# The last 128 columns of the final token block as a piece of their own, accumulated at the very end

## The chip, the cores and the metric

The kernel runs on one core of one Trainium2 chip. The time is the device time of one execution in microseconds (us), as the median of several executions. The profile's span is about 1.8 us shorter than the device time of the same execution, because it counts from the first to the last recorded instruction.

Ratios are the mean time of one kernel's runs over the mean time of the other's runs of the same rounds, so they are not quite the ratios of the medians that stand beside them.

## The reference

A linear attention (8 batches, 8 heads, 576 tokens, head size 64) feeds an MLP with a swish activation. The change touches only the last product of the MLP.

```python
kv  = einsum('bhsd,bhse->bhde', softmax_over_s(k), v)
x   = einsum('bhsd,bhde->bhse', softmax_over_d(q), kv)   # -> 4608 tokens x 512
h   = x @ w_in                                           # 512 -> 2048
g   = h * sigmoid(beta * h)
out = g @ w_out                                          # 2048 -> 512, float32
```

## The kernel before

Tokens are handled in blocks of 512 (R = 4 groups of 128 rows). For each block, 16 units of 128 hidden features (NJ = 16) each go through four matmuls into an h bank (a bank is one piece of PSUM, the memory into which matmuls write), a tanh on ScalarE, a product on VectorE that gives `g`, and then the second product: each unit adds `g` times `w_out` into accumulators of 512 columns. In the last block (LASTC), units 0 to 7 (HOLD = 8) are added inside the loop, and units 8 to 15 at the end, one accumulator after the other, so that the copies and stores of the first accumulators lie beside the matmuls of the later ones. The fourth group of rows is split into two accumulators of 256 columns, so that the last copy and the last store are half as large:

```python
def mm_b(c, j, sts=None):
    acc = acc_tiles(c)            # last block: 5 accumulators, acc[3] and acc[4] for the 4th row group
    ...
        if c == LASTC and st >= R - 1:
            hw = DM // 2          # 256 columns
            nc.tensor.matmul(acc[st][:, 0:hw], g[:, ds((R - 1) * P, P)],
                             w_out_b[:, j, ds((st - R + 1) * hw, hw)],
                             start=(j == 0), stop=(j == NJ - 1))
    ...
def store(c, st):                 # last block, st >= R - 1
    k_ = st - R + 1
    cols = ds(k_ * hw, hw)
    evac((nc.vector, nc.scalar)[k_], o[:, R - 1, cols], acc[st][:, 0:hw])
    (nc.sync, nc.scalar)[k_].dma_start(ov[:, R - 1, cols], o[:, R - 1, cols])
...
# after the loop: units 8 to 15 of each accumulator of the last block
for st in range(1, R + 1):
    for j in range(HOLD + (st == 1), NJ):
        mm_b(LASTC, j, [st])
    store(LASTC, st)
```

The softmax here doesn't subtract the row's maximum and nothing guards it: scores larger than these inputs give would overflow.

## Time and profile before

| | before |
|---|---|
| device time, median (first three runs) | 282.67 us (281.89 to 282.89) |
| span of the profiled run | 280.6 us |
| TensorE busy | 275.9 us, 98% |
| last matmul's end | 277.45 us |
| last matmul's end to the end of the span ("the tail") | 3.13 us |

The first rows say that TensorE sets the time. In the profile lines of this document, L and a number is a line of the kernel that was run, an arrow points from what is read to what is written, "x16" counts instructions, and PEld is the weight load that goes ahead of each matmul. The view lines for this kernel stand in the prediction below.

### The profile page before, as it was taken

The numbers are of one execution on the slowest core, as the hardware profiler recorded it, in microseconds if no ns is written. First come the engines' busy times: TensorE is split into PE (matmuls) and PEld (weight loads), VectorE is DVE, ScalarE is ACT, GpSimd is POOL, SyncE is SP. The second block draws the span as 40 slices with busy tenths as digits, with TensorE's granted clock in tenths as the row PEclk, the third lists the DMA queues.
The fourth block names the chain that finished last, engine by engine and source line by source line (L and its number), as shares of the span: only waits on it lengthen the run. The fifth ranks groups of instructions, "written<-read, shape, count | busy, mean of one in ns | idle before, by whom it ended". The sixth has DMA issues, their size and how long they took to land.

```text
span 280.6 us, 4450 instructions
## 1 busy us (share of the span) xinstructions
PE 275.9 (98%) x1728; PEld 128.6 (46%) x1728; DVE 175.1 (62%) x284; ACT 162.8 (58%) x248; POOL 38.7 (14%) x58
## 2 busy tenths in 40 slices
PE   8999999999999999999999999999999999999995
PEld 2544454444444444444444444444444544445543
DVE  3864796994478446945595549553864596354361
ACT  4667985958486447744684559444733574454451
POOL 1554236133030003000300030000000000000000
PEclk9999999999999999999999999999999999999999
DMA  7999999999981993199418951641154034005003
GB/s 249 390 394 391 387 388 311 321 292 213 269 240 46 238 287 90 75 233 265 141 78 191 280 167 75 132 94 79 71 89 139 1 151 75 0 0 152 0 0 150
DMA packets 55172, 50.09 MB, mean 179 GB/s; under 512 B 26600, under 2 KB 47344, under 8 KB 55152
## 3 DMA queue, kind: packets, MB, share of 16 engines
q1 hardware_dynamic: 54224, 48.91, 59.8%
q10 hardware_dynamic: 928, 0.92, 0.9%
q8 instruction: 13, 0.21, 0.3%
q14 instruction: 7, 0.06, 0.1%
HBM read 36.71 MB, written 9.44 MB: 164 GB/s over the span
## 4 chain that ended last, share of the span: by engine, by line
PE 98%; DVE 1%; ACT 0%; issue 0%
PE h L403 44%; PE acc L452 43%; PE warm L531 3%; PE kv L341 2%; PE x L372 1%; PE acc L444 1%; PE kv L316 1%; PE x L388 1%; PE tp L297 1%; DVE eq L267 0%; DVE qsT L173 0%; ACT o L171 0%; DVE xT L612 0%; PE x L363 0%; PE tb L564 0%
## 5 line engine op out<-in xcount | busy, mean ns | idle before, releaser
L417 DVE SCALAR_TENSOR_TENSOR g<-th,h 128x512 bf16<-128x512 bf16 x144 | 96.2, 681 | 80.1 <-ACT th L413 79.8
L413 ACT ACTIVATE th<-h,beta_t 128x512 bf16<-128x512 f32 x144 | 97.9, 687 | 81.9 <-PE h L403 81.0
L403 PE MATMUL h<-xT,w_in_b 128*128 128x512 bf16 x576 | 143.2, 379 | 0.0
L452 PE MATMUL acc<-w_out_b,g 128*128 128x512 bf16 x560 | 141.0, 379 | 0.0
L403 PEld LDWEIGHTS <-w_in_b 128*128 128x128 bf16 x576 | 56.3, 98 | 66.4 <-ACT w_in_b L171 0.6
L452 PEld LDWEIGHTS <-g 128*128 128x128 bf16 x560 | 53.8, 98 | 66.0 <-issue 2.5
L173 POOL CAST va<-v_st 128x2048 bf16<-128x2048 f32 (+2 forms) x14 | 17.4, 1257 | 115.2 <-DMA v_st<-in_v_dram 115.2
L261 DVE TENSOR_REDUCE rq<-eq 128x16 f32<-128x1024 bf16 (+1 forms) x20 | 22.1, 1104 | 5.6 <-ACT eq L250 5.1
L267 DVE TENSOR_TENSOR eq<-eq,rq 128x1024 bf16<-128x1024 bf16 (+1 forms) x20 | 23.1, 1157 | 0.1
L171 ACT CAST xT<-x 128x512 bf16<-128x512 f32 x18 | 9.9, 588 | 17.8 <-PE x L372 14.9
L250 ACT ACTIVATE eq<-q_st 128x1024 bf16<-128x1024 f32 (+1 forms) x18 | 16.9, 955 | 2.9 <-DMA q_st<-in_q_dram 2.9
L173 DVE COPY o<-acc 128x512 f32<-128x512 f32 (+1 forms) x19 | 12.3, 660 | 3.6 <-PE acc L452 3.4
L171 ACT COPY o<-acc 128x512 f32<-128x512 f32 (+1 forms) x18 | 9.6, 577 | 8.4 <-PE acc L452 5.0
L173 DVE CAST xT<-x 128x512 bf16<-128x512 f32 x18 | 11.5, 684 | 2.5 <-PE x L372 1.8
L192 ACT ACTIVATE ek<-k_st 128x1024 bf16<-128x1024 f32 x12 | 12.6, 1051 | 0.0
L531 PE MATMUL warm<-xT 128*128 128x512 bf16 x30 | 10.0, 493 | 1.2 <-DVE xT L612 1.2
L173 POOL CAST w_in_b<-w_in 128x512 bf16<-128x512 f32 (+1 forms) x9 | 5.9, 663 | 4.9 <-DMA w_in<-in_moe_w_in_dram 4.7
L531 PEld LDWEIGHTS <-xT 128*128 128x128 bf16 x30 | 3.5, 122 | 6.1 <-issue 3.8
L173 POOL CAST w_out_b<-w_out 128x1024 bf16<-128x1024 f32 x5 | 5.2, 1041 | 7.4 <-DMA w_out<-in_moe_w_out_dram 7.4
L262 DVE RECIPROCAL rq<-rq 128x16 f32<-128x16 f32 (+1 forms) x20 | 4.9, 243 | 0.7
L341 PEld LDWEIGHTS <-ek 128*64 128x64 bf16 x192 | 4.1, 111 | 2.5 <-issue 2.5
L185 ACT ACTIVATE ek<-k_st 128x576 bf16<-128x576 f32 x8 | 5.1, 677 | 0.2 <-DMA k_st<-in_k_dram 0.2
(48 smaller groups left out, 83.1 us busy)
## 6 DMA issues: line engine op xcount, KB each, us to landing
out_dram<-o SPq DMA_DIRECT2D x14, 512.0 KB, 3.4
q_st<-in_q_dram SPq DMA_DIRECT2D x25, 256.0 KB, 4.2
k_st<-in_k_dram SPq DMA_DIRECT2D x6, 1024.0 KB, 9.2
v_st<-in_v_dram SPq DMA_DIRECT2D x6, 1024.0 KB, 11.3
w_in<-in_moe_w_in_dram SPq DMA_DIRECT2D x6, 512.0 KB, 9.6
v_st<-in_v_dram SPq DMA_DIRECT2D x8, 288.0 KB, 8.3
w_out<-in_moe_w_out_dram SPq DMA_DIRECT2D x4, 512.0 KB, 9.0
w_out<-in_moe_w_out_dram SPq DMA_DIRECT2D x2, 1024.0 KB, 9.3
```

The source lines that it names most:

```text
L171: eng.copy(dst, src)
L173: eng.tensor_copy(dst, src)
L192: nc.scalar.activation(ek[b][:, :, h, :].rearrange("p i h d -> p h i d"), k_st[b][:, h, 0 : R * D].rearrange("p h (i d) -> p h i d", i=R), ...
L250: nc.scalar.activation(eq[b][:, :, s * m : (s + 1) * m, :].rearrange("p i h d -> p h i d"), q_st[b][:, s * m : (s + 1) * m, :].rearrange(" ...
L261: nc.vector.tensor_reduce(rq[b][:, 0, :, h], eq[b][:, :, h, :], axis=AX.X, op=ALU.add)
L267: eng.tensor_tensor(eq[b][:, :, h, :], eq[b][:, :, h, :], rq[b][:, 1, :, h].unsqueeze(3).to_broadcast((P, R, m, D)), ALU.mult,)
L341: nc.tensor.matmul(t[r * D : (r + 1) * D, j, :], ek[b][:, i, hd, :] if i < R else ekt[(b // 2) % 2][:, ds(hd * D, D)], va[b][:, i, hd, :] ...
L403: nc.tensor.matmul(h[:], w_unit(j, kt), x_of(c)[:, kt, :], start=(kt == 0), stop=(kt == KT - 1),)
L413: nc.scalar.activation(th[:], h_of[c, j][:], ACTF.Tanh, scale=beta_t[:, j : j + 1])
L417: nc.vector.scalar_tensor_tensor(out=g[:], in0=th_of.pop((c, j))[:], scalar=1.0, in1=h_of[c, j][:], op0=ALU.add, op1=ALU.mult)
L452: nc.tensor.matmul(acc[st][:], g[:, ds(st * P, P)], w_out_b[:, j, :], start=(j == 0), stop=(j == NJ - 1),)
L531: nc.tensor.matmul(t[:], xT[2][:, 0, 0:P], xT[2][:, 0, :])
```

## The change

The intent is to make the work after the last matmul smaller. The fourth row group is divided into 256, 128 and 128 columns. The last 128 are not accumulated in the loop at all: when everything else is done, all 16 units are added at once in a bank that held h tiles and is free by then, and the result is copied by ScalarE and stored from ScalarE's queue. While those matmuls run, the store ahead can leave.

```diff
+    ENDS = ((0, DM // 2), (DM // 2, DM // 4), (3 * DM // 4, DM // 4))
@@ mm_b
-                hw = DM // 2
+                lo, hw = ENDS[st - R + 1]
...
-                    w_out_b[:, j, ds((st - R + 1) * hw, hw)],
+                    w_out_b[:, j, ds(lo, hw)],
@@ store
-                hw = DM // 2
-                k_ = st - R + 1
-                cols = ds(k_ * hw, hw)
-                evac((nc.vector, nc.scalar)[k_], o[:, R - 1, cols], acc[st][:, 0:hw])
-                (nc.sync, nc.scalar)[k_].dma_start(ov[:, R - 1, cols], o[:, R - 1, cols])
+                lo, hw = ENDS[st - R + 1]
+                cols = ds(lo, hw)
+                last = st == R - 2 + len(ENDS)
+                evac(nc.scalar if last else nc.vector, o[:, R - 1, cols], acc[st][:, 0:hw])
+                (nc.scalar if last else nc.sync).dma_start(ov[:, R - 1, cols], o[:, R - 1, cols])
@@ the end
-    for st in range(1, R + 1):
-        for j in range(HOLD + (st == 1), NJ):
+    for st in range(1, R + 2):
+        if st > R:
+            acc_of[LASTC].append(ps.tile([P, DM], F32, tag=bank("h"), bufs=1, name=f"acc{LASTC}_{st}"))
+        for j in range(HOLD + (st == 1) if st <= R else 0, NJ):
             mm_b(LASTC, j, [st])
```

## The prediction

> **What bounds the kernel now.** I read the page's busy table first, then the chain that ended last, then the groups by form, then the timeline of the last 5 us, and last the stretches of the final store. The page and the chain, in order of time, say that one engine sets the time from start to end:
>
> ```profile
> PE 275.9 (98%) x1728; PEld 128.6 (46%) x1728; DVE 175.1 (62%) x284; ACT 162.8 (58%) x248; POOL 38.7 (14%) x58
> ...
> PE 98%; DVE 1%; ACT 0%; issue 0%
> ...
> 265.34 5.18 PE h L403 x24
> 270.52 5.18 PE acc L452 x24
> 275.70 1.76 PE acc L444 x16
> ```
>
> The first line is busy time, the second the chain by engine, the rest the end of the chain (start, length, count). TensorE is busy for 98% of a span of 280.6 us, and it is also what the chain runs through. So a change is worth what it takes off the matmul stream, plus what it takes off the stretch after the last matmul. That stretch is the target of the change, and the timeline has it:
>
> ```profile
> 275.54 1.91 PE L444 MATMUL acc<-w_out_b,g 128*128 128x256 bf16 x16
> 275.74 0.69 DVE L173 COPY o<-acc 128x512 f32<-128x512 f32 x1 [2.55 <-PE acc L452]
> 276.46 0.33 SPq L515 DMA_DIRECT2D out_dram<-o  x1
> 276.62 0.42 DVE L173 COPY o<-acc 128x256 f32<-128x256 f32 x1 [0.18 <-PE acc L444]
> 277.07 0.33 SPq L512 DMA_DIRECT2D out_dram<-o  x1
> 277.49 0.37 ACT L171 COPY o<-acc 128x256 f32<-128x256 f32 x1 [2.89 <-PE acc L444]
> ...
> 277.89 0.36 ACTq L512 DMA_DIRECT2D out_dram<-o  x1
> ```
>
> The last matmul ends at 275.54 + 1.91 = 277.45. ScalarE copies its 128x256 half from 277.49 to 277.86, its queue issues the store at 277.89, and the DMA list gives 1.8 us from that issue to landing, which is 279.7. The last 0.9 us to 280.6 is the ending of the program. So the tail after the last matmul is 280.6 - 277.45 = 3.15 us. This is 1.1% of the span: even its whole removal wouldn't reach the 2% line, 5.65 us.
>
> **What the Trainium skill says.** "TensorE: Matmul & The Clock Gate", section "Back-to-back issue gap", has N/2.4 + 2.5 ns for a warm matmul of N columns, but also says that a real stream of weight load and matmul pairs sustains about 81 ns at N=128. The two differ for the new matmuls: 55.8 against 81. This trace agrees with the formula at N=256: the 16 matmuls above span 1.91 us with a last one of 273 ns, so (1.91 - 0.273)/15 = 109 ns each, and the formula has 109.2. At N=128 with a fresh 128x128 weight load each, the trace has the transposes of L297, and at N=64 the L363 group:
>
> ```profile
> 40.45 0.45 PEld L297 LDWEIGHTS <-eq 128*128 128x128 bf16 x8
> 40.45 0.62 PE L297 MATMUL tp<-identity,eq 128*128 128x128 bf16 x8
> ...
> 217.90 0.40 PE L363 MATMUL x<-qsT,kvp 128*128 128x64 bf16 x8
> ```
>
> (0.62 - 0.219)/7 = 57 ns, and (0.40 - 0.193)/7 = 30 ns, where 219 and 193 ns are one instruction of each from the groups by form. So the trace agrees with the formula, not with 81; and full weight loads that alternate with 64-column matmuls keep up with 30 ns although one is recorded as 98 ns long. I take 56 ns. "DMA: Bandwidth & Descriptors", section "Anatomy of one DMA", puts a fixed ~2.0 us on a DMA, most of it the write receipt, independent of size (for the GpSimd path); the trace has 1.8 us for the final 128 KB store on ScalarE's queue, of the same order. The same page, section "Why small descriptors are slow", gives about 3 cycles of overhead on top of one per 32 bytes, for the packet cost used below.
>
> **The change part by part.** The last token block's fourth quarter of rows used to be two accumulators of 256 columns, each accumulated for units 0 to 7 inside the main loop and for 8 to 15 at the end. Now it is 256, 128 and 128 columns; the last 128 are taken out of the loop and done for all 16 units at the very end, in an h bank. The built instruction order shows 32 more TensorE rows (16 weight loads, 16 matmuls) and the new group last.
>
> Removed on TensorE: the second accumulator's 16 matmuls narrow from 256 to 128 columns, 8 in the loop and 8 at the end: 16 x (109 - 56) = 0.85 us. The loop part, 8 x 53 = 0.42 us, counts in full only if TensorE doesn't wait there; the stretches 250 to 260 and 260 to 270 us show it busy 10.00 of 10.00 us each.
> Added on TensorE: 16 matmuls of 128 columns, 16 x 56 = 0.90 us.
> Sum: +0.05 us by these rounded figures. The total number of columns is the same; what is added is 16 times the fixed 2.5 ns, 0.04 us. The last matmul itself records 219 instead of 273 ns, but that is already in the pace. So TensorE ends at about 277.5, against 277.45.
>
> Last copy: 128x128 instead of 128x256 on ScalarE. The groups by form have both sizes on each engine:
>
> ```profile
> L171 ACT COPY o<-acc 128x512 f32<-128x512 f32 x17 | 9.3, 589 | 5.5 <-PE acc L452 5.0
> ...
> L171 ACT COPY o<-acc 128x256 f32<-128x256 f32 x1 | 0.4, 372 | 2.9 <-PE acc L444 2.9
> ...
> L173 DVE COPY o<-acc 128x512 f32<-128x512 f32 x18 | 11.9, 673 | 3.4 <-PE acc L452 3.4
> ...
> L173 DVE COPY o<-acc 128x256 f32<-128x256 f32 x1 | 0.4, 425 | 0.2 <-PE acc L444 0.2
> ```
>
> ScalarE: 256 columns cost 589 - 372 = 217 ns, so 128 more or fewer cost 108, and the new copy is 372 - 108 = 264 ns, estimated. On the path: -0.11 us. VectorE's new 128-column copy is about 425 - 124 = 301 ns; it lies beside the 0.9 us of new matmuls and is off the path.
>
> Last store: 64 KB in 512-byte rows instead of 128 KB in 1024-byte rows. In stretches of 0.1 us the old one shows as
>
> ```profile
> 278.70:278.80 0.10, 0.00 (x0) 1.00 0.22 82
> 278.80:278.90 0.10, 0.00 (x0) 1.00 0.90 328
> 278.90:279.00 0.10, 0.00 (x0) 1.00 0.98 358
> 279.00:279.10 0.10, 0.00 (x0) 1.00 0.98 358
> 279.10:279.20 0.10, 0.00 (x0) 1.00 0.50 164
> 279.20:279.30 0.10, 0.00 (x0) 1.00 0.08 21
> ```
>
> where the last two columns are the share of the 16 DMA engines and GB/s. The shares sum to 3.66 tenths, 0.37 us of each engine. By the skill's packet rule 1024 bytes are 32 + 3 = 35 cycles and 512 bytes 16 + 3 = 19, so the new store needs 0.37 x 19/35 = 0.20 us, an estimate: -0.17 us. The issue before it (0.8 us) and the receipt behind it (about 0.4 us) stay.
>
> The earlier stores don't collide. The 128 columns taken out of the loop move the ends of the other accumulators 0.42 us forward. The third one's copy then ends near 276.6 and the fourth's (128 columns on VectorE) near 276.95, so the sync queue issues at about 276.65 and 277.0, and the last issue, on ScalarE's queue, comes at about 277.8. Before, the last two issues were 277.07 and 277.89.
>
> Sum on the path: +0.05 (matmuls) - 0.11 (copy) - 0.17 (store) = -0.23 us. One more store has its completion waited for at the end, perhaps +0.03. So about -0.2 us: 282.67 - 0.2 = 282.45.
>
> **The rivals.** *First, weight loads become the pace.* If 32 matmuls of 128 columns run at the skill's sustained 81 ns, they cost 32 x 25 = 0.8 us more, and the time is about 283.25; at the recorded 98 ns of a load it is 32 x 42 = 1.3 us, 283.8. For it: the weight load's record, and the skill's figure for such streams. Against it: the transposes' 57 ns and the 30 ns at 64 columns. One chance in ten.
> *Second, a wait for the new bank.* The new accumulator takes a bank that held an h tile, and its first matmul must wait until ScalarE and VectorE have read that tile. The last such read ends at 271.97 in the timeline (the last g), and the new group begins near 276.6: 4.6 us of slack, so this wait should be nothing. Nor should the operands bind: the last group needs the 16 g tiles of the block, and the last of these is the same one. If the bank did bind for a reason that the profile doesn't show, it would cost a few tenths. One in twenty.
> *Third, the gain is wholly hidden.* If the end is set by fixed store latency, halving the last store returns nothing beyond the copy, and an extra completion at the end costs a little: 282.6. The stretches speak for part of this: 0.2 us of about 1.8 us from issue to landing is all that depends on size. One in four. All these differ by less than the three runs of before do among themselves (281.89 to 282.89), so the total alone will hardly tell them apart; the profile should.
>
> **Range and chances.** The centre is 282.45. The mechanisms span -0.25 to +1.1 us, mostly below zero; the spread of runs adds half a microsecond either way to a median. I take 281.8 to 283.1. For 2% the time would have to leave 277.0 to 288.3, and no mechanism here comes near: faster 0.005, same 0.99, slower 0.005.
>
> **What would show it.** Right: in the profile of after, the 128x128 matmuls of the second line of accumulators number 32 and their last 24 span 23 x 56 + 219 = 1.5 us; no idle time of TensorE before them; TensorE's end within 0.1 us of 277.5; the last ScalarE copy about 264 ns; the last store landing about 1.6 us after its issue; and a span of about 280.4. Wrong: a 24-group of 2.1 us or more (weight loads bind), a wait ahead of the new accumulator's first weight load (the bank), a last landing of 1.8 us or more (fixed latency), or a loop that doesn't get its 0.42 us shorter. A total outside the range with these lines all as foretold would mean that the end of the program, after the last landing, has changed.

## The result and the profile after

The changed kernel took 281.98 us (median of four, 281.92 to 282.13) against 282.50 us of the kernel before in the same rounds (281.89 to 282.89). The ratio is 0.9984, with a 95% interval of 0.9965 to 1.0004. That is within 2% by far, and the interval still holds 1. The predicted 282.45 us is 0.47 us above the median, and inside the range.

Busy times and the chain by engine, from the page of the changed kernel:

```profile
PE 275.6 (98%) x1744; PEld 128.7 (46%) x1744; DVE 175.3 (63%) x285; ACT 162.6 (58%) x248; POOL 38.3 (14%) x58
...
PE 95%; DMA 3%; POOL 1%; SPq 0%; issue 0%; ACT 0%
```

The 16 new matmuls are there (1744 against 1728) and TensorE is as busy as it was. The chain now has 3% of DMA in it. That is at the start of the program, where the chain followed back from the end runs into a load of `v` (the page's chain by line has it as v_st), ahead of anything that the change touches.

The end of the chain in order of time (start, length, count), changed kernel:

```profile
264.65 5.18 PE h L404 x24
269.83 5.18 PE acc L453 x24
275.01 2.23 PE acc L445 x32
```

TensorE still leads to the end; only its last group has grown from 16 to 32 matmuls.

The last 3 us, from the timeline of the changed kernel:

```profile
274.85 2.38 PE L445 MATMUL acc<-w_out_b,g 128*128 128x256 bf16 x32
275.05 0.69 DVE L174 COPY o<-acc 128x512 f32<-128x512 f32 x1 [2.55 <-PE acc L453]
275.92 0.74 DVE L174 COPY o<-acc 128x256 f32<-128x256 f32 x2 [0.18 <-PE acc L445]
276.37 0.83 SPq L513 DMA_DIRECT2D out_dram<-o  x2
277.26 0.27 ACT L172 COPY o<-acc 128x128 f32<-128x128 f32 x1 [3.35 <-PE acc L445]
277.56 0.36 ACTq L513 DMA_DIRECT2D out_dram<-o  x1
```

The first line merges 8 matmuls of 256 columns and 24 of 128 under the shape of the first. With the 109 ns of a 256-column one and 219 ns for the last, the 128-column ones come every (2.38 - 8 x 0.109 - 0.219)/23 = 0.056 us. The last matmul ends at 277.22, the copy takes 265 ns by the trace's record (372 before), and the store is issued at 277.56. The two earlier pieces are copied and issued well ahead of that.

The final store in stretches of 0.1 us (share of the 16 DMA engines and GB/s in the last two columns), changed kernel:

```profile
278.40:278.50 0.10, 0.00 (x0) 1.00 0.39 123
278.50:278.60 0.10, 0.00 (x0) 1.00 0.95 292
278.60:278.70 0.10, 0.00 (x0) 1.00 0.72 210
278.70:278.80 0.10, 0.00 (x0) 1.00 0.14 31
```

The shares sum to 2.2 tenths, 0.22 us of each engine, where before they summed to 0.37. The list of DMA issues has a last column with the time from issue to landing. The final store of the kernel before, then of the changed kernel:

```profile
out_dram<-o ACTq DMA_DIRECT2D x1, 128.0 KB, 1.8
```

```profile
out_dram<-o ACTq DMA_DIRECT2D x1, 64.0 KB, 1.6
```

The two profiles divide at three instructions. The first is the start of the h matmuls of the last block's units 1 and 2, the last matmuls ahead of the first changed one; I call it the mark. The times below are the trace's own records to the nanosecond, rounded to 10; "last landing" is the last increment of the final store's semaphore. Further below, the spread of a store is the time from the start of its first packet to the end of its last, and its receipt the time from there to its landing.

| stretch | before | after | difference |
|---|---|---|---|
| start to the mark | 250.49 | 250.22 | -0.27 |
| from the mark to the last matmul's end | 26.97 | 27.01 | +0.04 |
| last matmul's end to the last landing | 2.28 | 1.96 | -0.32 |
| last landing to the end of the span | 0.85 | 0.94 | +0.09 |
| span | 280.59 | 280.13 | -0.46 |

The change can act only on the last three rows, which sum to -0.19 us. The first row is a stretch in which both kernels have the same instructions. So two questions stay: is that -0.27 us chance, and does the -0.32 + 0.09 us come about as the prediction has it?

### The profile page after: what moved, and what is told of

It is laid out like the page before. It is cut to its first block, busy times and chain, and to the rows that moved or that the text cites. A ratio compares the mean times of both kernels' runs of the same rounds, so it can differ in the third digit from the quotient of the medians.

```text
span 280.1 us, 4485 instructions
## 1 busy us (share of the span) xinstructions
PE 275.6 (98%) x1744; PEld 128.7 (46%) x1744; DVE 175.3 (63%) x285; ACT 162.6 (58%) x248; POOL 38.3 (14%) x58
## 4 chain that ended last, share of the span: by engine, by line
PE 95%; DMA 3%; POOL 1%; SPq 0%; issue 0%; ACT 0%
PE h L404 44%; PE acc L453 44%; DMA v_st<-in_v_dram 3%; PE kv L342 2%; PE x L373 1%; PE acc L445 1%; PE kv L317 1%; PE x L389 1%; POOL va L174 1%; PE tp L298 0%; SPq L132 0%; SPq L109 0%; ACT o L172 0%; PE x L364 0%; PE tb L565 0%
## 5 line engine op out<-in xcount | busy, mean ns | idle before, releaser
L174 DVE COPY o<-acc 128x512 f32<-128x512 f32 (+2 forms) x20 | 12.6, 642 | 3.6 <-PE acc L453 3.4
L532 PE MATMUL warm<-xT 128*128 128x512 bf16 x30 | 9.4, 469 | 1.2 <-DVE xT L613 1.2
```

Of the source, the lines that this page charges most:

```text
L174: eng.tensor_copy(dst, src)
L532: nc.tensor.matmul(t[:], xT[2][:, 0, 0:P], xT[2][:, 0, :])
```

## The experiments

My theory was that only the tail counts: a smaller copy and a smaller last store gain, one completion more costs, and the move out of the loop gains nothing by itself but gives the stores ahead time to leave. The rivals were that the move itself gains, that a narrow last piece is all that counts, and that the store's latency is fixed and its size returns nothing. Eight runs followed, four on one chip and four on another; each four share their own runs of the kernel before. bigstore took part in only three rounds, so its ratio rests on fewer of them than the median beside it.

| run | median us | before, same batch | ratio [95%] | tail us | to last landing | landing to end |
|---|---|---|---|---|---|---|
| before | | | | 3.13 | 2.28 | 0.85 |
| changed kernel, first | 281.98 | 282.50 | 0.9984 [0.9965, 1.0004] | 2.91 | 1.96 | 0.94 |
| rerun | 281.96 | 282.27 | 0.9990 [0.9977, 1.0002] | 2.89 | 1.95 | 0.95 |
| nomove | 282.52 | 282.27 | 1.0002 [0.9988, 1.0016] | 3.37 | 2.52 | 0.85 |
| movealone | 282.35 | 282.27 | 0.9998 [0.9986, 1.0011] | 3.13 | 2.29 | 0.84 |
| narrow64 | 282.25 | 282.27 | 0.9996 [0.9983, 1.0010] | 3.03 | 2.08 | 0.96 |
| bigstore | 281.97 | 282.14 | 0.9999 [0.9984, 1.0015] | 3.03 | 2.18 | 0.85 |
| merge | 281.69 | 282.14 | 0.9988 [0.9975, 1.0000] | 2.80 | 1.96 | 0.84 |
| afterdrop (wrong result) | 281.78, one run | 282.14 | none | 2.80 | 1.95 | 0.85 |
| narrow64drop (wrong result) | 281.36, one run | 282.14 | none | 2.64 | 1.79 | 0.85 |

The last three columns are from each run's trace. They repeat to 0.02 us where the same kernel was profiled twice (2.91 and 2.89), while the timed runs of one kernel spread over 0.2 to 1.0 us. No ratio here is clear of 1.

### rerun: the changed kernel again

There is no edit.

> The changed kernel again, unaltered, to learn how much of the first comparison's 0.45 us is the change. In the two traces the stretch from the start of the last token block's first matmul (250.65 before, 250.38 after) to the last matmul's end is 26.80 against 26.84 us, and the stretch from the last matmul's end to the end of the span is 3.13 against 2.91 us; the other 0.27 us arises before the first changed instruction. Theory (only the tail counts): ratio 0.9993 to the kernel before (-0.19 us), with an interval that holds 0.9993, and a profile with 2.9 us after the last matmul. Rival (the change also speeds up something ahead of the tail): ratio 0.9984 again (-0.45 us).

The ratio came out at 0.9990, between the two expectations, with an interval that holds 0.9993 as well as 0.9984. The tail repeated (2.89 us). The mark is at 250.27 us in this trace; in nomove, movealone and narrow64, which all have the same instructions up to there, at 250.47, 250.08 and 250.42. So the mark varies by 0.4 us between executions with the same instructions up to it (249.93 to 250.49 over all ten traces), and the -0.27 us of the first comparison is inside that. The kernel before has only one trace, and its mark is the latest of the ten; how far it scatters by itself can be estimated from its 18 timed runs in the two later batches. Their spans are 280.0 to 281.1 us, and less the 30.10 us that lie behind the mark in its trace this puts the mark between 249.9 and 251.0 us. (The expectation gives 250.65 and 250.38 for before and after and calls the mark the last block's first matmul; those times are from the chain, which starts the merged group later, and unit 0 in fact comes just before it. The difference is the same.) That the change gains exactly 0.19 us of device time isn't shown by the timed runs: they only don't contradict it.

### nomove: a narrow last piece, without the move

```diff
+    ENDS = ((0, 3 * DM // 4), (3 * DM // 4, DM // 4))      # 384 and 128 columns
-                hw = DM // 2                                # in mm_b and store, against the kernel before
+                lo, hw = ENDS[st - R + 1]
```

> The kernel before with its two last accumulators made 384 and 128 columns wide instead of 256 and 256; nothing moved out of the loop, no third accumulator, no extra store. TensorE's work is equal (16 x (162 + 56) against 16 x 218 ns). The last copy is the changed kernel's (about 265 ns) and the last store its 64 KB. Theory that the move out of the loop matters because it lets the stores ahead drain: here 192 KB is copied in about 0.55 us beside 0.45 us of matmuls, issued about 0.15 us after the last matmul, its packets start about 1.0 us after it and share the DMA engines with the last store's, so the last packet ends about 1.8 us after the last matmul as in the kernel before, the tail stays at 3.05 to 3.15 us, ratio 1.000. Rival (a narrow last piece is all that counts): tail 2.85 to 2.9 us, ratio 0.9990 to 0.9993.

The tail was 3.37 us: not the gain of the rival, and even 0.24 us longer than in the kernel before. The timeline of nomove:

```profile
277.03 0.56 DVE L174 COPY o<-acc 128x384 f32<-128x384 f32 x1 [0.61 <-PE acc L445]
277.47 0.27 ACT L172 COPY o<-acc 128x128 f32<-128x128 f32 x1 [2.89 <-PE acc L445]
277.62 0.33 SPq L513 DMA_DIRECT2D out_dram<-o  x1
277.77 0.36 ACTq L513 DMA_DIRECT2D out_dram<-o  x1
```

The last copy and its issue are as early as in the changed kernel (0.33 us after the last matmul), but the 192 KB store ahead is issued only 0.15 us before the 64 KB one. By the trace its packets run from 278.45 to 279.12, and the last store's, which could have begun at about 278.64 (0.87 us from issue to first packet, as in the changed kernel), run from 278.98 to 279.34. They land 2.2 us after their issue, not 1.6. So a narrow last piece alone is worth nothing here. (The piece ahead also grew, to 384 columns. Pieces of 256, 128 and 128 columns without the move were not run; merge below shows that a store of 384 columns does no harm when it leaves early enough.) I had the mechanism right but too small: I expected the last packet 1.8 us after the last matmul, and it came at 1.90; the landing took 0.62 us more, where 0.47 had been seen before.

### movealone: the move, without a narrower piece

```diff
     # acc_tiles: no fifth accumulator in the loop
-                acc_of[c].append(ps.tile([P, DM], F32, tag=bank("att"), ...))
-                AB[:] = [AB[turns["att"] % 2]] * 2
     # the end
+        if st == R:
+            acc_of[LASTC].append(ps.tile([P, DM], F32, tag=bank("h"), ...))
-        for j in range(HOLD + (st == 1), NJ):
+        for j in range(HOLD + (st == 1) if st < R else 0, NJ):
```

> The kernel before with its last 256 columns taken out of the loop and accumulated over all 16 units at the very end in an h bank, but not narrowed: the move without the split. Theory: the loop loses 8 x 109 ns and the end gains 8 x 109 ns, so 26.8 us from the last block's first matmul to the last matmul's end as before; the store ahead of the last one is issued 0.87 us earlier, but it did not collide in the kernel before either (its last packet ended 0.26 us before the last store's first), so the tail stays 3.1 us and the ratio is 1.000. Rival (the move itself gains, by a shorter loop or earlier stores): 0.2 us or more less, ratio 0.9993 or below; rival (the h bank makes TensorE wait): idle time before the last group and a ratio above 1.001.

The tail is that of the kernel before (3.13 us), and from the mark to the last matmul's end it is 27.01 against 26.97 us. The loop's lighter units are paid back at the end. The new bank brought no wait: the profile's list of waits has no wait of a matmul for it. The 0.04 us is a pause elsewhere. By the trace, one h matmul near the end of the loop starts 259 ns after the one before it instead of 215 or 216, at 264.81, just after a VectorE product that reads an h tile has ended at 264.76: that fits a wait for an h bank that was not yet free, in a loop whose units are now lighter. The trace of the changed kernel has no such pause. The move gains nothing by itself, as expected.

### narrow64: pieces of 256, 192 and 64 columns

```diff
-    ENDS = ((0, DM // 2), (DM // 2, DM // 4), (3 * DM // 4, DM // 4))
+    ENDS = ((0, DM // 2), (DM // 2, 3 * DM // 8), (7 * DM // 8, DM // 8))
```

> The changed kernel with its last three pieces 256, 192 and 64 columns wide instead of 256, 128 and 128. TensorE: same columns and same number of matmuls, 16 of them at about 29 ns, so within 0.02 us of the changed kernel up to the last matmul. Tail: last copy about 210 ns instead of 265; last store 32 KB in 256-byte rows. If the time of a packet goes on falling with its size, the spread of the last store's packets falls from 0.35 to about 0.25 us and the tail is about 2.75 us, ratio 0.9995 to the changed kernel. Rival (fixed latency and small packets return nothing): only the copy's 0.05 us, tail 2.85 us or more. Rival (weight loads bind below 128 columns): the last 16 matmuls take 16 x 56 ns and the last matmul comes 0.4 us later.

The matmul part came as expected: the group spans 2.16 us, and with 8 x 109 ns and 8 x 82 ns for the wider ones (the second is the step between them in the trace, 82 or 83 ns) and 193 ns for the last, the narrow ones come every (2.16 - 0.87 - 0.66 - 0.19)/15 = 0.029 us. The copy took 212 ns. But the tail was 3.03 us, not 2.75: longer than in the changed kernel, so the expectation of the theory fell. The stretches of narrow64:

```profile
278.50:278.60 0.10, 0.00 (x0) 1.00 0.67 210
278.60:278.70 0.10, 0.00 (x0) 1.00 0.87 208
278.70:278.80 0.10, 0.00 (x0) 1.00 0.63 131
278.80:278.90 0.10, 0.00 (x0) 1.00 0.06 10
```

There is no gap between the two stores. The 16 narrow matmuls take 16 x 29 ns = 0.47 us of TensorE instead of 16 x 56 ns = 0.89, so the store of 192 columns is issued only 0.04 us before the last matmul's end; its packets run to 278.68, while the last store's begin at 278.58. The last packet ends at 278.86, but the landing is at 279.51, 0.65 us later, against 0.41 in the changed kernel. From this one run it could be the neighbour or the 256-byte rows; narrow64drop tells them apart.

### narrow64drop: the same without the store of the 192 columns

```diff
+                if st == R:
+                    return          # the fourth piece is not stored: a wrong result on purpose
                 (nc.scalar if last else nc.sync).dma_start(...)
```

> The kernel with pieces of 256, 192 and 64 columns, without the store of the 192 columns (a wrong result on purpose). That kernel's tail was 3.03 us instead of the 2.75 expected: its last packets started 0.1 us before the store ahead ended theirs, and the receipt took 0.65 us behind the last packet instead of 0.41. Theory (the store ahead delays the receipt): with it gone the receipt takes about 0.42 us, the last landing comes at about 1.82 us instead of 2.08, and the tail is about 2.67 us. Rival (256-byte rows have a slow receipt of their own): receipt still 0.65 us, landing at about 2.05 us, tail about 2.9 us.

The result was wrong. The stretches of narrow64drop:

```profile
278.10:278.20 0.10, 0.00 (x0) 1.00 0.78 182
278.20:278.30 0.10, 0.00 (x0) 1.00 0.60 123
278.30:278.40 0.10, 0.00 (x0) 1.00 0.05 8
```

The last packet ends at 278.34 and the landing is at 278.73, 0.38 us later; the last landing comes 1.79 us after the last matmul (expected 1.82) and the tail is 2.64 us (expected 2.67). So the 256-byte rows have no slow receipt of their own, and the store ahead cost narrow64 the 0.29 us. Nearly all of it is in the receipt: the last packet ended 1.43 us after the last matmul with the neighbour and 1.41 without. This has a ground in the Trainium skill: "DMA: Bandwidth & Descriptors", section "Queues, rings and completion order", says that the semaphore increment is a strongly ordered write, which lands only after every earlier write of that DMA engine, across its queues. Traces agree with that order: in narrow64 the store ahead landed at 279.33 and the last store at 279.51. They don't show that the rule is the whole cause. By the rule alone the last store could have landed with the store ahead, at 279.33, since its own packets and a receipt of 0.38 us would have had it land at 279.24; it came 0.18 us later. The store ahead, itself close behind another store, had a receipt of 0.65 us too. So writes that back up after several stores in a row would fit as well, and no run separates the two.

### bigstore: the small copy with a store of the old size

```diff
+                if st == R:
+                    return          # the fourth piece goes out with the fifth
+                cols = ds(DM // 2, DM // 2) if last else cols
                 (nc.scalar if last else nc.sync).dma_start(...)
```

> The changed kernel, but the fourth piece's 128 columns are not stored on their own: they go out with the last 128 columns, as one store of 128 KB in 1024-byte rows after the last copy. The copy stays small, the store is as large as in the kernel before, and there are five stores as before instead of six. Theory (the size of the last store counts): its packets spread over about 0.51 us as before instead of 0.35, so the last landing comes about 2.12 us after the last matmul (changed kernel 1.96, before 2.28); from there to the end 0.85 us as before (changed kernel 0.94, because it waits for one store more), so a tail of about 2.97 us. Rival (fixed latency): landing at 1.96 us and a tail of 2.81 us.

The last copy from the timeline of bigstore, and its final store from the list of DMA issues:

```profile
277.08 0.27 ACT L172 COPY o<-acc 128x128 f32<-128x128 f32 x1 [3.35 <-PE acc L445]
```

```profile
out_dram<-o ACTq DMA_DIRECT2D x1, 128.0 KB, 1.8
```

The last landing came 2.18 us after the last matmul, 0.06 later than expected, and 0.22 later than in the changed kernel, with the same copy (266 ns) and the same delay to the issue. The packets spread over 0.51 us and the receipt took 0.47, as in the kernel before (0.51 and 0.47; changed kernel 0.35 and 0.41). So the size of the last store is worth 0.22 us, of which 0.16 are packets and 0.06 receipt, and the rival of a fixed latency is out. (bigstore also has one store fewer ahead of the last; afterdrop, below, shows that this doesn't move the landing.) The rest, 2.28 - 2.18 = 0.10 us, is the copy.

### afterdrop: the changed kernel without its fourth piece's store

The edit is that of narrow64drop, made in the changed kernel; the result is wrong.

> The changed kernel without the store of the fourth piece (128 columns stay unwritten: a wrong result on purpose). Theory (in the changed kernel the store ahead is out of the way, only its completion costs): last landing 1.95 us after the last matmul as in the changed kernel, tail 2.80 instead of 2.90 us because one completion fewer is waited for. Rival (that store also delays the last one): landing 1.85 us or earlier.

The landing stays at 1.95 us: in the changed kernel the store ahead is out of the way. The tail is 2.80 us, because the stretch after the landing is 0.85 instead of 0.94 us. The waits of the sync engine's queue at the end, in the kernel before and in the changed kernel (total, times, longest):

```profile
SPq L983 <- DMA out_dram<-o: 2.0, 2, 1.4
```

```profile
SPq L986 <- DMA out_dram<-o: 1.8, 1, 1.8
```

Before, the queue waits for the stores one after the other and the last store's wait is the last. With the sixth store, it waits for the last store first, in one long wait, and takes up the others after it. By the trace, its closing instruction comes 0.08 us after the last landing before, and 0.19 us after it in the changed kernel. Every run with six stores has 0.94 to 0.96 us from landing to end, and every run with five has 0.84 to 0.85. In the changed kernel's trace the last store is on the semaphore that the queue waits for third from last, and the two waits behind it, for stores long landed, add 0.13 us (279.207 to 279.334). That the order of the waits is the reason is my reading of the trace; that the sixth store goes with the cost is what the runs show.

### merge: the two pieces ahead of the last stored together

```diff
+                if st == R - 1:
+                    return                                     # stored with the next piece
+                cols = cols if last else ds(0, 3 * DM // 4)    # 384 columns in one store
                 (nc.scalar if last else nc.sync).dma_start(...)
```

> The changed kernel, but the two pieces ahead of the last are stored together, 384 columns and 192 KB in one store after the fourth piece's copy; the last piece is as in the changed kernel. Theory (the sixth store's completion costs 0.10 us at the end, and a store only delays the last one if its packets or receipts are still under way): the merged packets run from about 0.3 to 0.95 us after the last matmul, the last store's first packet comes at 1.2 us, so the last landing stays at 1.95 us and the end comes 0.85 instead of 0.94 us later: tail 2.80 us, ratio 0.9996 to the changed kernel. Rival (192 KB just ahead slows the last store's receipt as 384 columns did in the run without the move): landing at 2.1 us or later, tail 2.95 us or more.

The last landing stayed at 1.96 us and the tail is 2.80 us, both as expected. The timeline of merge:

```profile
276.54 0.33 SPq L516 DMA_DIRECT2D out_dram<-o  x1
277.11 0.27 ACT L172 COPY o<-acc 128x128 f32<-128x128 f32 x1 [3.35 <-PE acc L445]
277.41 0.36 ACTq L516 DMA_DIRECT2D out_dram<-o  x1
```

The same 192 KB that made nomove longer does no harm here. It is issued 0.87 us before the last store instead of 0.15, because 16 matmuls of 128 columns lie between, and its packets are over 0.24 us before the last store's begin. The result is correct, and the median, 281.69 us, is 0.45 us below that of the kernel before in the same rounds. Its tail is the shortest of the correct kernels, 0.33 us under the kernel before and 0.10 under the changed one. That it beats the changed kernel in device time was not measured on one chip, and 0.1 us would not show beside the spread of the runs.

## Why the prediction was right

The outcome was right (within 2%, inside the range), but by the total alone that says little, since the range was wider than the change and the runs' spread larger too. What the prediction can be held to is the sum on the path: -0.20 us foretold, -0.19 measured from the mark to the end. The steps hold with these sizes:

- **Matmuls**, +0.05 foretold, +0.04 measured from the mark to the last matmul's end (of the size of the prediction's 16 x 2.5 ns; movealone's equal 0.04 us is its pause and not this). The pace of 56 ns at 128 columns was right; narrow64 shows 29 ns at 64, so the rival of binding weight loads is out. The loop did get shorter by its 0.42 us: the chain has the loop's h groups 1.67 to 1.68 us apart in the changed kernel (for example 259.62 and 261.30), and 1.73 before.
- **Copy**, -0.11 foretold, 265 against 372 ns measured.
- **Store**, -0.17 foretold for the packets, -0.16 measured as their spread; of each engine the new store took 0.22 us and not 0.20. The receipt fell by another 0.06 us (0.47 to 0.41), which the prediction had as constant at about 0.4.
- **Stores ahead don't collide**: right, and it turned out to be the condition of the whole gain. Afterdrop shows no delay left; nomove and narrow64 show what it costs when the condition is missed.
- **One completion more**, +0.03 foretold, +0.09 to +0.10 measured: this term was too small by a factor of three. The prediction gave no ground for it, and the profile before has no run with six stores to read it from. That the sum still came out is luck in this part: the 0.06 us by which the receipt fell unforeseen and the 0.06 us by which this term was too small cancel.
- **Rivals**: the wait for the bank did not occur. The hidden gain, which I gave one chance in four, is ruled out by bigstore.

Two of the marks that I set were missed: TensorE's end "within 0.1 us of 277.5" was 277.22, and the span "about 280.4" was 280.1. Both are 0.3 us off for one reason: they are counted from the start of the span, and the mark, ahead of every changed instruction, varies by up to 0.4 us between the first six traces. I should have set them from there. That the median lies 0.47 us below the predicted 282.45 is not explained by the tail either, whose 0.2 us is already in the prediction. 0.17 us of it is the starting point: the prediction started from 282.67, and with a fourth run the median of the kernel before is 282.50. The rest is of the size of the runs' own spread, and no run here attributes it to the change.

## What to carry to other kernels

The last piece of work should be small in bytes but long enough in compute: it must cover the copy and departure of the store ahead, or the last store waits behind it. Here, cutting the last piece finer than that made the tail 3.03 us instead of 2.91, and cutting it without moving work behind the store ahead made it 3.37 instead of 3.13. Where a gain is far below the spread of timed runs, measure stretches that start and end at named instructions on either side of the change, and ask whether a store added at the end can be carried by an existing one: here that saved 0.10 us.

## What the Trainium skill lacked or had wrong

- "TensorE: Matmul & The Clock Gate", section "Back-to-back issue gap", gives about 81 ns for each matmul in a sustained stream of weight load and matmul pairs at N=128. Here such pairs, each with a full 128x128 load, ran at 56 ns at 128 columns and 29 ns at 64, which is the section's own formula N/2.4 + 2.5, given there for a single matmul on its own. At 512 columns the section has about 131 ns in such a stream; here 24 of them took 5.18 us, 216 ns each.
- "DMA: Bandwidth & Descriptors", section "Specifications", puts the least transfer for line rate at 512 bytes and speaks of a read-modify-write below. The final store of narrow64drop in 256-byte rows took 0.15 us of the engines (the sum of its stretches and the one before them) for 32 KB, against 0.22 for 64 KB in 512-byte rows and 0.37 for 128 KB in 1024-byte rows. By these shares the 512-byte rows, too, ran below the pace of the longer ones (about 300 against 360 GB/s, and 220 for the 256-byte rows, all estimates), and nothing else shows at 256 bytes: the receipt was no slower (0.38 against 0.41 us).
- The same page, section "Queues, rings and completion order", has the rule that an increment lands after the engine's earlier writes, but no figure for what that costs. Here the last store's receipt took 0.38 to 0.47 us on engines that were free and 0.62 to 0.65 us close behind another store. The section "Anatomy of one DMA", which the prediction cites, makes the receipt most of about 2.0 us on the GpSimd path; on ScalarE's queue the 1.84 us of the kernel before divide into 0.86 to the first packet, 0.51 of packets and 0.47 of receipt.
- No page that I read has the cost of one more store at the end of a program: 0.09 to 0.10 us between the last landing and the end here.
